# The last two half-width matmuls of an attention decode kernel change places

## The chip, the cores and the metric

The kernel runs on one core of a Trainium2 chip. The metric is the device time of one execution in microseconds (us). A profile comes from one profiled execution; its span is the time from the first to the last instruction, about 2 us less than the device time.

## The reference, cut to what matters

Two attention blocks, A and B, decode one token for four batch rows. A attends to 8192 cached positions, B to the last 2048. Each ends in a projection, and the two results stand side by side.

```python
def _A_ref(x, k_cache, v_cache, wq, wo):            # x: (4, 1, 512), Hq = 32, Hkv = 8, Dh = 128
    q = (x @ wq).reshape(B, Sq, Hq, Dh) ...
    scores = einsum("bhqd,bhkd->bhqk", q, k) * Dh ** -0.5
    o = einsum("bhqk,bhkd->bhqd", softmax(scores), v)
    return o.transpose(0, 2, 1, 3).reshape(B, Sq, Hq * Dh) @ wo
# _B_ref: the same on the last W = 2048 positions
return concatenate([a, b], axis=-1)                  # (4, 1, 1024), bf16
```

## The kernel before

The kernel streams 184.56 MB of keys, values and weights from HBM and works through them in 20 units. The change concerns the very end: the last eight heads (C = 8) of A's projection, whose output is 4 rows of D = 512 columns. The columns are split into two halves of H2 = 256, each accumulated in a PSUM bank of its own. `halves[0]`, called SA in the profile, is copied out by VectorE and sent by SyncE's DMA queue; `halves[1]`, called KT, is copied out by ScalarE and sent by ScalarE's own queue. Every head waits for its own 128 KB piece of the weights (`("WL", i)`).

```python
        halves = [SA[(L + 1) % 2][0:Bn, 0:H2], KTB[2][0:Bn, 0:H2]]
        # ... (cut: seed with the earlier heads' sums, values of the last unit, normalisation)
        for i, n in enumerate(WCH):                  # WCH = [1] * C
            for hq in range(h0, h0 + n):
                for hf in (1, 0):                    # ScalarE's half, then VectorE's
                    def lfn(pe, hq=hq, hf=hf):
                        return pe.matmul(out=halves[hf], lhsT=OT_sb[:, 0, NSEG - 1, hq, :],
                                         rhs=Wl_sb[:, hq, hf * H2:(hf + 1) * H2],
                                         start=False, stop=(hq == C - 1))
                    op("pe", lfn, waits=[("WL", i), ("otr", L), ("oc", L - 1)], inc=("fin", hf) if hq == C - 1 else None)
            h0 += n
        op("dve", lambda dve: dve.tensor_copy(out=osb[:, 0, 0:H2], in_=halves[0]), waits=[("fin", 0)], inc=("ocp", NTURN))
        op("act", lambda act: act.activation(out=osb[:, 0, H2:D], in_=halves[1], func=ACTF.Copy), waits=[("fin", 1)], inc=("Ef",))
        op("act", dma(out[:, 0, H2:D], osb[:, 0, H2:D]), waits=[("Ef",)], inc=("out", 2))
        # ... (cut)
        op("sp", dma(out[:, 0, 0:H2], osb[:, 0, 0:H2]), waits=[("ocp", NTURN)], inc=("out", 0))
        # ... and SyncE's last step: wait for the landing of outputs 1, 2 and 0
```

## Time and profile before

| What | Value |
|---|---|
| device time, first 3 runs | 439.19 us median (438.82 to 439.37) |
| span of the profile | 437.0 us |
| DMA engines at 0.9 or more | 38 of 40 slices |
| start of the last pair of matmuls | 434.47 us |
| last output landed | 436.546 us |

The load stream fills the span; what follows its end, from the last pair of matmuls to the last output's landing, takes 2.07 us. The prediction shows the lines. Three words are used throughout. An **eviction** is the copy of a finished half from its accumulator (PSUM) into SBUF. An **issue** is the instruction by which SyncE or ScalarE hands a transfer to the DMA engines. A transfer reports that it is complete by incrementing a semaphore, a counter on which engines can wait; the last of these increments is its **landing**. Landings are not rows of the timeline: they are read from the trace's record of semaphore increments, to the nanosecond, and so are the starts of packets. From here on the **tail** is the time from the start of the first matmul of the last pair to the last landing of an output. It leaves out when the load stream ends, which differs from run to run.

### The profile page before, as it was taken

What the parts mean: (1) busy time and instruction counts of PE and PEld (TensorE: products, weight loads), DVE (VectorE), ACT (ScalarE), POOL (GpSimd) and SP (SyncE); (2) the same over time, 40 slices, a digit from 0 to 9 for tenths busy, and PEclk for the clock granted to TensorE, in tenths of its full rate; (3) what the DMA queues carried; (4) which work ended last, traced back from release to release, by engine and by line L of the source; (5) the groups of instructions that cost most, each with busy time, mean ns of one, the idle gap of its engine ahead of it and who ended that gap; (6) DMA issues with size and microseconds to landing.
All of it is one profiled execution on the core that took longest, in us unless ns stands there. A gap on an engine that the chain in (4) does not pass through costs nothing.

```text
span 437.0 us, 15525 instructions
## 1 busy us (share of the span) xinstructions
PE 365.0 (84%) x7174; PEld 337.9 (77%) x7184; DVE 210.0 (48%) x406; ACT 195.0 (45%) x249; POOL 27.7 (6%) x88
## 2 busy tenths in 40 slices
PE   0168898998998959895989598969868996989996
PEld 0158897997997949795979588868868886979975
DVE  0004455664564634563456247525643563455651
ACT  1024473573653625371634254434534462536530
POOL 6100000000000000000000000000100000000000
PEclk9999999999999988999999899989996999799999
DMA  8999999999999999999999999999999999999996
GB/s 340 430 421 421 429 412 430 418 439 412 445 432 432 424 438 432 432 432 432 432 432 429 432 432 430 431 433 432 410 454 432 432 432 432 432 432 411 447 407 255
DMA packets 10996, 184.73 MB, mean 423 GB/s; under 512 B 1236, under 2 KB 2280, under 8 KB 2408
## 3 DMA queue, kind: packets, MB, share of 16 engines
q1 hardware_dynamic: 10960, 184.56, 99.1%
q8 instruction: 8, 0.13, 0.1%
q14 instruction: 4, 0.03, 0.0%
q10 hardware_dynamic: 24, 0.01, 0.0%
HBM read 184.56 MB, written 0.01 MB: 422 GB/s over the span
## 4 chain that ended last, share of the span: by engine, by line
PE 54%; DMA 40%; issue 2%; DVE 1%; SPq 1%; ACT 1%
DMA K_sb<-in_A_k_cache_dram 29%; PE KT L283 27%; PE OT L338 11%; DMA K_sb<-in_B_k_cache_dram 7%; PE SB L322 5%; PE SA L322 4%; DMA V_sb<-in_A_v_cache_dram 4%; PE KT L396 4%; PE SA L350 1%; PE KT L338 1%; SPq L566 1%; DVE oacc L404 1%; PE KT L263 1%; ACT KT_sb L299 1%; DVE OS L501 0%
## 5 line engine op out<-in xcount | busy, mean ns | idle before, releaser
L283 PE MATMUL KT<-identf,K_sb 128*128 128x128 f32 x1280 | 207.6, 296 | 44.1 <-DMA K_sb<-in_A_k_cache_dram 30.7
L299 ACT ACTIVATE KT_sb<-KT 128x1024 bf16<-128x1024 bf16 (+1 forms) x192 | 165.1, 881 | 120.6 <-PE KT L283 120.6
L283 PEld LDWEIGHTS KT<-identf,K_sb 128*128 128x128 f32 x1280 | 147.6, 150 | 49.3 <-DMA K_sb<-in_A_k_cache_dram 31.7
L299 DVE COPY KT_sb<-KT 128x512 int32<-128x512 int32 x160 | 110.5, 691 | 132.1 <-PE KT L283 130.7
L338 PE MATMUL OT<-PT,V_sb 128*128 128x64 bf16 x2560 | 78.1, 193 | 1.6 <-issue 1.1
L338 PEld LDWEIGHTS OT<-PT,V_sb 128*128 128x128 bf16 x2560 | 75.9, 98 | 1.8 <-issue 1.2
L469 ACT ACTIVATE PT<-Dt 128x512 bf16<-128x512 f32 x40 | 24.6, 630 | 84.0 <-DVE Dt L458 84.0
L322 PEld LDWEIGHTS SA<-RQc,KT_sb 128*128 128x128 bf16 x1280 | 56.9, 98 | 2.3
L322 PEld LDWEIGHTS SB<-RQc,KT_sb 128*128 128x128 bf16 x1280 | 51.1, 97 | 7.9 <-issue 4.4
L322 PE MATMUL SA<-RQc,KT_sb 128*128 128x16 bf16 x1280 | 56.4, 170 | 0.0
L322 PE MATMUL SB<-RQc,KT_sb 128*128 128x16 bf16 x1280 | 52.9, 170 | 0.0
L420 DVE TENSOR_REDUCE M<-SB 128x8 f32<-128x512 f32 (+1 forms) x20 | 13.8, 692 | 50.0 <-PE SB L322 50.0
L441 POOL PARTITION_ALL_REDUCE MB<-M1m x20 | 7.7, 387 | 334.3 <-DVE M1m L434 334.3
L396 PE MATMUL KT<-Wo_sb,OL 128*4 128x512 bf16 x80 | 18.9, 379 | 0.0
L201 PE MATMUL KT<-ident,x_sb 4*128 4x4 bf16 x8 | 0.6, 170 | 19.9 <-POOL identf L537 19.9
L201 PEld LDWEIGHTS KT<-ident,x_sb 4*128 4x128 bf16 x8 | 0.4, 112 | 20.1 <-issue 20.1
L476 DVE TENSOR_REDUCE LB<-SA 128x8 f32<-128x512 f32 (+1 forms) x20 | 13.7, 684 | 2.8 <-PE SA L350 2.8
L458 DVE TENSOR_TENSOR Dt<-SA,MBm 128x512 f32<-128x512 f32 x20 | 13.8, 692 | 0.7
L367 DVE TENSOR_TENSOR ORx<-KT,MSK 32x1024 bf16<-32x1024 bf16 x10 | 12.1, 1211 | 3.3 <-PE KT L362 3.3
L458 DVE TENSOR_TENSOR Dt<-SB,MBm 128x512 f32<-128x512 f32 x20 | 13.6, 681 | 0.0
L420 DVE TENSOR_REDUCE M<-SA 128x8 f32<-128x512 f32 (+1 forms) x20 | 13.6, 681 | 0.0
L350 PE MATMUL SA<-PT,onesb 128*128 128x128 bf16 x168 | 12.7, 218 | 0.0
(69 smaller groups left out, 118.0 us busy)
## 6 DMA issues: line engine op xcount, KB each, us to landing
K_sb<-in_A_k_cache_dram SPq DMA_DIRECT2D x15, 4096.0 KB, 22.5
V_sb<-in_A_v_cache_dram SPq DMA_DIRECT2D x15, 4096.0 KB, 30.3
K_sb<-in_B_k_cache_dram SPq DMA_DIRECT2D x8, 2048.0 KB, 23.6
V_sb<-in_B_v_cache_dram SPq DMA_DIRECT2D x16, 1024.0 KB, 18.4
V_sb<-in_B_wq_dram SPq DMA_DIRECT2D x1, 4096.0 KB, 12.5
V_sb<-in_A_wq_dram SPq DMA_DIRECT2D x1, 4096.0 KB, 21.8
Wo_sb<-in_B_wo_dram SPq DMA_DIRECT2D x4, 1024.0 KB, 11.9
K_sb<-in_A_k_cache_dram SPq DMA_DIRECT2D x2, 2048.0 KB, 17.5
```

The costliest lines, as they stand in the source:

```text
L283: ins = pe.transpose(out=bkf[:, pi * 128:(pi + 1) * 128], in_=K_sbf[:, slot, t0:t0 + 2, :].rearrange("p t d -> p (t d)"), identity=identf[ ...
L299: ins = e.tensor_copy(out=d, in_=r) if eng == "dve" else e.activation(out=d, in_=r, func=ACTF.Copy)
L322: ins = pe.matmul(out=stb[:, t % NTH * C:(t % NTH + 2) * C], lhsT=ktv[:, pi, :, e], rhs=RQc[:, u % 2, t // TS, e, :], start=(e == 0), stop ...
L338: ins = pe.matmul(out=otb[:, s * NW:s * NW + w], lhsT=V_sb[:, slot, t, :], rhs=PT[:, slot, t * C:t * C + w], start=(j == 0), stop=(j == n ...
L350: ins = pe.matmul(out=SA[u % 2][:, s * NM:(s + 1) * NM], lhsT=onesb[:, :], rhs=PT[:, u % 2, c0:c0 + NM], start=(i == 0), stop=(i == n - 1))
L367: return dve.tensor_tensor(out=ORx[:, :, :, :], in0=bk[0:NR, 0:128].rearrange("p (i o r) -> p r o i", o=1, r=C).broadcast_to([NR, C, C, 12 ...
L396: ins = pe.matmul(out=bk[0:Bn, 0:D], lhsT=OL[:, i, :], rhs=Wo_sb[:, i, :], start=(i == 0), stop=(i == C - 1))
L420: return dve.tensor_reduce(out=M1[:, h * n:(h + 1) * n].rearrange("p (s h) -> p s h", h=C), in_=bank[:, :].rearrange("p (s j h) -> p s h j ...
L441: return pool.partition_all_reduce(MB[:, 0:n], M1m[:, 0:n], channels=128, reduce_op=ReduceOp.max)
L458: return dve.tensor_tensor(out=Dt[:, h * NTH * C:(h + 1) * NTH * C].rearrange("p (s j h) -> p s j h", s=Sh, h=C), in0=bank[:, :].rearrange ...
L469: return act.activation(out=PT[:, u % 2, a:b], in_=Dt[:, a:b], func=ACTF.Exp, scale=scale)
L476: return dve.tensor_reduce(out=LB[:, 0:n].rearrange("p (s h) -> p s h", h=C), in_=SA[u % 2][:, 0:NSEG * NM].rearrange("p (s j h) -> p s h ...
```

## The change

The intent: VectorE's way from accumulator to output is the slower one, so its half should be ready first, ahead of ScalarE's. Only the last head is turned round.

```diff
-                for hf in (1, 0):
+                for hf in (1, 0) if hq < C - 1 else (0, 1):
```

## The prediction

> **What bounds the kernel now.** I read the page first: span, slices, chain.
>
> ```profile
> span 437.0 us, 15525 instructions
> ...
> DMA  8999999999999999999999999999999999999996
> ...
> HBM read 184.56 MB, written 0.01 MB: 422 GB/s over the span
> ...
> PE 54%; DMA 40%; issue 2%; DVE 1%; SPq 1%; ACT 1%
> ```
>
> The DMA engines are at 0.9 or more in 38 of the 40 slices; the two others are the first and the last. So nearly all of the 437 us is the time that 184.56 MB take to arrive. The chain has TensorE in 54% of its steps, but TensorE is paced by those loads. The change touches neither the loads nor anything ahead of the last two matmuls, so the whole argument lies in the last three microseconds. I read those in the timeline from 434.4 us on:
>
> ```profile
> 434.47 0.08 PEld L700 LDWEIGHTS KT<-Wl_sb,OT_sb 128*4 128x4 bf16 x1 [0.23 <-DMA Wl_sb<-in_A_wo_dram]
> 434.47 0.27 PE L700 MATMUL KT<-Wl_sb,OT_sb 128*4 128x256 bf16 x1
> 434.48 0.08 PEld L700 LDWEIGHTS SA<-Wl_sb,OT_sb 128*4 128x4 bf16 x1
> 434.58 0.27 PE L700 MATMUL SA<-Wl_sb,OT_sb 128*4 128x256 bf16 x1
> 434.78 0.37 ACT L705 ACTIVATE osb<-KT 4x256 bf16<-4x256 f32 x1 [9.44 <-PE KT L700]
> 434.89 0.41 DVE L704 CAST osb<-SA 4x256 bf16<-4x256 f32 x1 [2.20 <-PE SA L700]
> 435.18 0.27 ACTq L566 DMA_DIRECT2D out_dram<-osb  x1
> 435.33 0.29 SPq L566 DMA_DIRECT2D out_dram<-osb  x1
> ```
>
> The columns are start, duration, engine, line, operation. KT holds the half of the columns that ScalarE evicts and sends on its own queue; SA holds the half that VectorE evicts and SyncE sends. The last pair of matmuls waits 0.23 us for the last piece of the output weights, so its start is set by the load stream. Then two branches run to the end side by side, the ScalarE one 0.11 us ahead. The chain of waits over the same stretch shows which ends last:
>
> ```profile
> 434.54 0.21 PE KT L700
> 434.74 0.12 PE SA L700
> 434.87 0.02 issue
> 434.89 0.41 DVE osb L704
> ```
>
> It goes through VectorE. The queue's own waits on SyncE close it:
>
> ```profile
> SPq L566 <- DVE osb L704: 7.4, 1, 7.4
> SPq L820 <- DMA out_dram<-osb: 0.9, 1, 0.9
> ```
>
> L820 is the final wait of the program, on both output transfers. SyncE's own issue ends at 435.33 + 0.29 = 435.62, and it then waits 0.9 us, so the outputs have landed near 436.5. The trace's record of semaphore increments gives the two apart: the ScalarE half's last increment at 436.362, the VectorE half's at 436.546. The wait ends at 436.56. The VectorE half is thus last by 0.184 us, and that slack is what a change of order can trade on. From 436.56 to 437.0 comes the closing handshake, the same for both kernels.
>
> **What the Trainium skill says.** Four places bear on it.
>
> "VectorE: DVE Perf Modes", section "The TRN2 errata", gives for PSUM to SBUF 120 + FD cycles at 0.96 GHz on VectorE and 172 + FD at 1.2 GHz on ScalarE. With 256 elements that is an estimate of 392 ns and 357 ns. The trace has 412 and 373: both some 5% longer, and VectorE slower by 39 ns against 35. The page agrees that the VectorE half is the slower one, so it should come first. I use the trace's durations.
>
> "Perfetto Trace Analysis", section "Tensor Engine Instruction (MATMUL, LD_WEIGHTS)", says that a matmul's reported end is computed and not observed. I therefore count from start to start of the evictions. These lie 434.89 − 434.78 = 0.11 us apart, as the matmuls do (434.58 − 434.47).
>
> The same page, section "DMA Instruction — HWDGE (DVE, Sync)", says that the descriptor generator is locked for exclusive use while an instruction generates descriptors, and that the data movement is not in the instruction's profiled window. The trace agrees on the second: an issue of 0.29 us has its last landing 1.2 us after its start. On the first no row of this trace decides: the two issues overlap (435.33 lies before 435.18 + 0.27 = 435.45) and the second takes 0.29 against 0.27.
>
> "DMA: Bandwidth & Descriptors", section "Issuing engines are not separate DMA queues", says that transfers issued from several engines run on the same 16 DMA engines and interleave. In the trace each output is four packets of 512 B, each packet 25 to 28 ns long, in 436.09 to 436.17 for SyncE's queue and 435.94 to 436.03 for ScalarE's. They do not overlap now.
>
> **The change part by part.** It removes nothing and adds nothing. On TensorE one matmul of 256 columns trades places with one other, with the same weights, and the static comparison of the two programs finds the other four engines unchanged. In the last of eight heads the SA matmul now runs first. Their order inside a bank's accumulation does not change, so the result should be bit for bit the same.
>
> The length of each branch, from the start of its eviction to the last landing:
> - VectorE branch: 434.890 to 436.546 = 1.656 us. It is made of 0.412 eviction, 0.029 to the issue (435.33 − 435.30), and 1.215 from the start of the issue to the landing.
> - ScalarE branch: 434.781 to 436.362 = 1.581 us: 0.373 eviction, 0.030 to the issue, 1.178 to the landing.
>
> The VectorE branch is longer by 0.075 us: 0.039 from the eviction and 0.037 from the transfer. Let the first eviction start at t, and the other at t + 0.109. Before, the end is t + 0.109 + 1.656 = t + 1.765 (VectorE), the other at t + 1.581. After, VectorE ends at t + 1.656 and ScalarE at t + 0.109 + 1.581 = t + 1.690. The later of these is t + 1.690, so the end comes 1.765 − 1.690 = **0.075 us earlier**. The whole 0.109 us of matmul spacing is not won, because ScalarE's branch becomes the last one after 0.075.
>
> What else moves: the last matmul of head 6 and the first of head 7 both now write SA, back to back. Before head 7 there is a 0.23 us wait for its weights, far longer than the 0.11 us spacing, so nothing can queue behind that. The accumulators are in separate banks, so VectorE's read of SA runs beside the KT matmul as ScalarE's read of KT runs beside the SA matmul now.
>
> Sum: −0.075 us of 439.19, which is 0.017%. The three runs before lie between 438.82 and 439.37, a spread of 0.55 us, seven times the gain.
>
> **The rivals.** First, **the two issues collide**. Now SyncE's issue begins 0.147 us after ScalarE's (435.331 − 435.184). After the change SyncE's begins at t + 0.441 and ScalarE's at t + 0.512, only 0.071 apart. If the descriptor generator serves one at a time, the second loses up to the added overlap of 0.147 − 0.071 = 0.076 us, which would eat the gain and leave 439.19. The packets would come 0.07 us apart as well, and each queue's four take about 0.09 us on the same DMA engines, a clash of at most 0.02 to 0.03 us. For it: the second issue is already 17 ns longer. Against it: the issues overlap today by 0.12 us with no more than those 17 ns lost. I give this a chance of one in four.
>
> Second, **VectorE stays the last**. If SyncE's transfer takes longer for being first, or its receipt comes late, the end stays on the VectorE branch at up to t + 1.765. To lose the whole gain it would have to lengthen by 0.109 us, for which no row speaks; between 0 and 0.109 us would be gained, so 439.08 to 439.19.
>
> Third, **the load stream decides by itself**. The time at which the last weights land (before 434.47) varies from run to run with 184.56 MB of transfers; 0.1% of the span is already 0.4 us. That does not hang on the order of two matmuls, but it can put the measured median either side of before. This is the likeliest thing to be seen, whatever happens in the tail: 438.8 to 439.4, as the three runs before.
>
> **Range and chances.** Prediction: 439.19 − 0.075, so 439.1 us. The range comes from the noise and not from the mechanism: the spread of 0.55 us over three runs, widened a little for another session, gives 438.5 to 439.7. Two per cent is 8.8 us, and the whole tail after the last matmuls is 2.5 us long; if all of it vanished the verdict would still be "the same". A loss of 2% would need a changed load stream. So faster 0.005, same 0.99, slower 0.005.
>
> **What would show it.** Right, if the timeline has the SA matmul at t' and KT 0.11 us later, the VectorE cast starting first and the ScalarE activation 0.11 us after it; SyncE's issue about 0.07 us ahead of ScalarE's; the ScalarE half's landing now the last, by about 0.03 us; and about 2.02 us from the first of the last pair of matmuls to the end of the final wait, where it is 436.56 − 434.47 = 2.09 now. The span itself may well move the other way. The collision is right if ScalarE's issue instruction is longer than 0.30 us, or its packets start more than 0.76 us after its issue began (435.94 − 435.18 now). The prediction is wrong if that tail is not shorter, or if the time leaves the range, which would point to the load stream.

## The result, and the profile after

The changed kernel takes 439.13 us (median of 6 runs, 438.84 to 439.68), the kernel before in the same rounds 439.11 (6 runs, 438.82 to 439.42). The ratio is 1.0002 with a 95% interval of 0.9989 to 1.0014. A ratio here is the mean time of one kernel's runs over that of the other's of the same rounds, so not quite the ratio of the two medians.

The page of the changed kernel has the same span and the same full DMA row:

```profile
span 437.0 us, 15535 instructions
...
DMA  8999999999999999999999999999999999999996
...
HBM read 184.56 MB, written 0.01 MB: 422 GB/s over the span
```

The timeline of its last microseconds (start, duration, engine, line, operation):

```profile
434.38 0.08 PEld L700 LDWEIGHTS SA<-Wl_sb,OT_sb 128*4 128x4 bf16 x1 [0.24 <-DMA Wl_sb<-in_A_wo_dram]
...
434.49 0.27 PE L700 MATMUL KT<-Wl_sb,OT_sb 128*4 128x256 bf16 x1
434.69 0.41 DVE L704 CAST osb<-SA 4x256 bf16<-4x256 f32 x1 [2.05 <-PE SA L700]
434.80 0.37 ACT L705 ACTIVATE osb<-KT 4x256 bf16<-4x256 f32 x1 [10.20 <-PE KT L700]
435.13 0.29 SPq L566 DMA_DIRECT2D out_dram<-osb  x1
435.20 0.27 ACTq L566 DMA_DIRECT2D out_dram<-osb  x1
```

The order is turned as intended: VectorE starts 0.11 us ahead, and SyncE's issue 0.07 us ahead of ScalarE's. The chain of waits, the last four pieces, now ends on ScalarE:

```profile
434.33 0.32 PE SA L700 x2
434.65 0.12 PE KT L700
434.78 0.02 issue
434.80 0.37 ACT osb L705
```

SyncE's own waits after the change:

```profile
SPq L566 <- DVE osb L704: 7.2, 1, 7.2
SPq L820 <- DMA out_dram<-osb: 1.1, 1, 1.1
```

The last line is what the forecast did not expect. The final wait starts when SyncE's issue is done, at 435.13 + 0.29 = 435.42, and takes 1.1 us, so the outputs have landed near 436.5, as before. The semaphore record has 436.492, against 436.546. That looks like a gain of 0.054 us, but the last pair of matmuls also started earlier, at 434.382 instead of 434.473, because its weights came earlier. The tail is 436.492 − 434.382 = 2.110 us, where it was 436.546 − 434.473 = 2.073. It got **longer by 0.037 us**; the forecast had it shorter by 0.075. One profile each does not tell a mechanism from scatter, so both are repeated first.

### The profile page after: what moved, and what is told of

The parts are those of the page before. It is cut to its first block, busy times and chain, and to the rows that moved or that the text cites. A ratio compares the mean times of both kernels' runs of the same rounds, so it can differ in the third digit from the quotient of the medians.

```text
span 437.0 us, 15535 instructions
## 1 busy us (share of the span) xinstructions
PE 366.5 (84%) x7184; PEld 338.5 (77%) x7184; DVE 209.9 (48%) x406; ACT 195.0 (45%) x249; POOL 27.7 (6%) x88
## 4 chain that ended last, share of the span: by engine, by line
PE 50%; DMA 40%; PEld 4%; issue 2%; DVE 1%; SPq 1%; ACT 1%; PEldq 0%
DMA K_sb<-in_A_k_cache_dram 29%; PE KT L283 25%; PE OT L338 10%; DMA K_sb<-in_B_k_cache_dram 7%; DMA V_sb<-in_A_v_cache_dram 4%; PE SB L322 4%; PE SA L322 4%; PE KT L396 3%; PEld KT L283 2%; PE SA L350 1%; PE KT L338 1%; SPq L566 1%; DVE oacc L404 1%; PEld OT L338 1%; PEld SA L322 1%
```

## The experiments

The two theories at the start. Theory 1: of two outputs sent close together, the later one is held back by the earlier one, and the tighter they come the more; the change brought them closer together. Theory 2: landings scatter by more than the 0.075 us in question.

**The same two kernels again**, no edit.

> The kernel before, once more, for its tail: from the start of the first matmul of the last pair to the last output landing (by the trace's semaphore records). It was 2.073 us in the first profile; the later output (VectorE's half, SyncE's queue) took 1.215 us from issue to landing. Theory 1, the later of two close outputs is delayed by the earlier one, in a repeatable way: 2.05 to 2.10 and 1.20 to 1.23 again. Theory 2, landings scatter from run to run by more than the 0.075 us forecast: the tail moves by over 0.05 us.

> The changed kernel, once more. Its first profile had a tail of 2.110 us, where the prediction had 2.073 - 0.075 = 2.00; the later output (ScalarE's half) took 1.289 us from issue to landing, where it took 1.178 when it was the earlier one. Theory 1 (a repeatable delay of the later output when the issues are only 0.07 us apart): 2.09 to 2.13 and 1.27 to 1.31 again. Theory 2 (scatter): the tail moves by over 0.05 us, towards 2.00. My prediction's step as it stood: 2.00 us and 1.18 us.

Measured: the kernel before has a tail of 2.068 us, the later output 1.211 from issue to landing. The changed kernel has 2.112 and 1.292. Both repeat within 0.005 us, in two profiles each. Theory 2 falls: the 0.04 us are real, and they are a loss. Each kernel from here on was profiled once. What does scatter is the load stream: over these four profiles the last pair starts between 434.38 and 434.64 us.

**A gap between the halves.** To see each branch alone, three matmuls with no use are put between the last two. In the changed kernel the condition is `hf == 0`.

```diff
+                    if hq == C - 1 and hf == 1:
+                        def gfn(pe):
+                            ins = None
+                            for _ in range(3):
+                                ins = pe.matmul(out=KTB[3][:, 0:512], lhsT=ident[:, :], rhs=RQ[0]..., start=True, stop=True)
+                            return ins
+                        op("pe", gfn)
```

> Three matmuls of 512 columns with no use are put between the last two matmuls of the projection (ScalarE's half first), so that the two outputs are some 0.65 us further apart and cannot touch each other. Measured is the branch from the start of VectorE's eviction to its landing. Theory 1: alone it takes 1.60 to 1.62 us, as it did when it was the earlier one in the changed kernel (1.612), not 1.656. Theory 2: anything from 1.56 to 1.68. Prediction's step as it stood: 1.656.

> The same three matmuls, VectorE's half first. Measured is the branch from the start of ScalarE's eviction to its landing. Theory 1: alone it takes 1.57 to 1.60 us, as when it was the earlier one in the kernel before (1.581), so that the pair with a gap shows the changed order ahead by only some 0.03 us (1.612 - 1.581) and not 0.075. Theory 2: anything from 1.53 to 1.70. Prediction's step as it stood: 1.581 and a difference of 0.075.

The timeline of the changed order with the gap shows the two ends apart:

```profile
434.68 0.41 DVE L712 CAST osb<-SA 4x256 bf16<-4x256 f32 x1 [2.09 <-PE SA L700]
...
435.12 0.29 SPq L566 DMA_DIRECT2D out_dram<-osb  x1
...
435.63 0.37 ACT L713 ACTIVATE osb<-KT 4x256 bf16<-4x256 f32 x1 [10.37 <-PE KT L700]
436.04 0.27 ACTq L566 DMA_DIRECT2D out_dram<-osb  x1
```

The issues are 0.92 us apart, which is 0.85 more than in the changed kernel and not 0.65. Alone, VectorE's branch from the start of its eviction to its landing takes 1.616 us (1.617 in the other gap kernel, where it came first) and ScalarE's takes 1.575 in both. From issue to landing the two transfers take the same, 1.177 and 1.172 to 1.173. So both numbers that the forecast used, 1.656 and 1.581, were of branches that met: the first held 0.04 us of waiting for the other output. What separates the branches is the eviction and little else, 0.041 us. With the gap the changed order is ahead by 2.880 − 2.838 = 0.042 us, a little more than the 0.03 expected, and not by 0.075.

It also shows a pattern. In both orders the later output lands a fixed time after the earlier one: 0.184 and 0.183 us in the two profiles of before, 0.188 and 0.187 in those of the changed kernel, although the issues are 0.147 us apart in one and 0.072 in the other. Alone they would land 0.148 and 0.068 us apart. For before that is 0.109 + 1.616 − 1.577, with the 1.577 that ScalarE's branch took as the earlier one in the second profile (1.581 in the first). For the changed kernel it is 0.109 + 1.575 − 1.616. The refined theory 1: the completions of two transfers come no closer than about 0.185 us, and a later one waits that out. This is not a spacing of any two increments: the four that follow the packets of one output come only 0.01 to 0.04 us apart. Taken one by one in their order, those of the later output follow those of the earlier by 0.177 to 0.188 us in these four profiles. Its rival: the second transfer, or ScalarE's, pays a fixed 0.115 us.

**A small delay** separates the two: one matmul of 4 x 192 with no use, between the last two of the changed kernel.

```diff
+                    if hq == C - 1 and hf == 0:
+                        op("pe", lambda pe: pe.matmul(out=KTB[3][0:Bn, 0:192], lhsT=OT_sb[:, 0, NSEG - 1, 0, :], rhs=Wl_sb[:, 0, 0:192],
+                                                      start=True, stop=True))
```

> In the changed kernel one matmul of 4x192 with no use stands between the last two, so that ScalarE's half comes some 0.08 us later. By the first runs an output alone lands 1.177 us after its issue, and of two close ones the later lands 0.183 to 0.188 us after the earlier. Theory 1 (completions are served one after the other, some 0.185 us apart): the later output's landing stays 0.185 us after the earlier one, so the tail to the last landing stays at 2.11 us although the last half is computed 0.08 later, and its time from issue falls from 1.29 to about 1.21. Rival (the delay belongs to ScalarE's queue being second, a fixed 0.115 us): 1.29 from issue again and a tail of 2.19.

```profile
434.81 0.41 DVE L707 CAST osb<-SA 4x256 bf16<-4x256 f32 x1 [2.06 <-PE SA L700]
435.00 0.37 ACT L708 ACTIVATE osb<-KT 4x256 bf16<-4x256 f32 x1 [9.89 <-PE KT L700]
435.25 0.29 SPq L566 DMA_DIRECT2D out_dram<-osb  x1
435.40 0.27 ACTq L566 DMA_DIRECT2D out_dram<-osb  x1
```

ScalarE's eviction now starts 0.19 us after VectorE's, 0.08 more than in the changed kernel. Its output takes 1.205 us from issue instead of 1.29, lands 0.187 after the other, and the tail is 2.107. Delaying the last half by 0.08 us cost nothing: that time had been spent waiting anyway. The fixed charge is out.

**What the later output waits for.** SyncE sends a load of the same shape in place of its output, and the output itself only after ScalarE's has landed.

```diff
-        op("sp", dma(out[:, 0, 0:H2], osb[:, 0, 0:H2]), waits=[("ocp", NTURN)], inc=("out", 0))
+        op("sp", dma(x_sb[0:Bn, 0, 0:H2], X[0][:, 0, 0:H2]), waits=[("ocp", NTURN)], inc=("out", 0))
+        op("sp", dma(out[:, 0, 0:H2], osb[:, 0, 0:H2]), waits=[("out", 2)], inc=("out", 3))
```

> The changed kernel, in which SyncE at the time of its output issues a load of the same shape (four rows of 512 B, from HBM to SBUF) in its place, and sends VectorE's half only after ScalarE's has landed (the result stays right, the end comes over 1 us later). Measured is ScalarE's output from issue to landing. If what holds it back is any earlier transfer on the same DMA engines that is not complete: 1.25 us or more, as behind an output (1.29). If it is the earlier write to HBM: near 1.18 as when alone.

```profile
435.35 0.27 SPq L566 DMA_DIRECT2D x_sb<-in_A_x_dram  x1
435.42 0.27 ACTq L566 DMA_DIRECT2D out_dram<-osb  x1
436.85 0.28 SPq L566 DMA_DIRECT2D out_dram<-osb  x1
```

The load lands 1.305 us after its issue, and ScalarE's output 1.420 after its own, which is 0.187 us after the load. Each transfer makes four increments after its packets, as many as it has rows; taken one by one, those of the output follow those of the load by 0.180 to 0.187. So the earlier transfer need not be a write to HBM: a load that is not complete holds the output back as another output does. The packets of the two run among each other here. The output's last one starts only 0.029 us after the load's last (436.340 and 436.311), and its landing still comes 0.187 after, so most of the distance arises after the packets.

**One transfer for both halves**, from ScalarE's queue, in either order.

```diff
-        op("act", dma(out[:, 0, H2:D], osb[:, 0, H2:D]), waits=[("Ef",)], inc=("out", 2))
+        op("act", dma(out[:, 0, 0:D], osb[:, 0, 0:D]), waits=[("Ef",), ("ocp", NTURN)], inc=("out", 2))
```

(SyncE's output transfer and the wait for it are taken out.)

> The changed order, but one output transfer of 4 KB, issued by ScalarE's queue when both halves are evicted, in place of two of 2 KB. Theory 1: no second completion to wait for, so issue to landing 1.18 to 1.21 and a tail of 2.00 to 2.03 us from the first matmul of the last pair to the last landing, some 0.05 us less than before (2.07) and 0.1 less than the changed kernel (2.11). Rival (it is the bytes or the rows that take the time, not the second completion): 1.29 and a tail of 2.11.

> The order of before with the same single transfer from ScalarE's queue. The issue now waits for VectorE's eviction, which ends last: 0.109 + 0.412 against 0.109 + 0.373 after the first eviction's start. Theory 1: tail 2.04 to 2.07 us, 0.04 longer than after_one: with one transfer the change of order is worth the 0.039 us by which the evictions differ. Rival as for after_one: 2.15.

This one missed. In the changed order the tail is 2.073 us and not 2.00 to 2.03: the transfer of four rows of 1 KB takes 1.254 us from issue to landing, 0.08 more than one of four rows of 512 B. There is no second completion, but the wider rows cost nearly as much: from the start of the first packet to the end of the last it is 0.167 us (436.053 to 436.220), where an output of 2 KB took 0.094 (435.940 to 436.034 in the first profile of before). It is level with the kernel before and 0.037 us better than the changed kernel. In the order of before the tail is 2.169, where 2.04 to 2.07 were expected and 2.15 by the rival. Of the 0.096 us more than the other order, 0.039 are the evictions' difference, as expected; the rest is that ScalarE's queue has the wait for VectorE as a step of its own: VectorE is done at 435.472, and the issue starts at 435.564.

**Uneven halves.** If completions need 0.185 us between them, it pays to let the first half end earlier, at the price of a longer second one, up to the point where the second one arrives just in time. VectorE's half becomes 208 of the 512 columns in the changed order, and 272 in the order of before.

```diff
-        halves = [SA[(L + 1) % 2][0:Bn, 0:H2], KTB[2][0:Bn, 0:H2]]
+        CUT = [0, 208, D]                     # [0, 272, D] in the order of before
+        halves = [SA[(L + 1) % 2][0:Bn, 0:CUT[1]], KTB[2][0:Bn, 0:D - CUT[1]]]
```

(and CUT in place of H2 in the matmuls, evictions and transfers)

> The changed order with VectorE's half cut to 208 columns and ScalarE's widened to 304. Estimate from the runs: a column costs 0.42 ns in the matmul (0.109 us for 256), and in the evictions about 1.04 ns on VectorE and 0.83 on ScalarE. VectorE's landing then comes 48 x 1.46 = 0.070 us earlier, at 1.85 us after the start of the first matmul of the last pair, and the later completion can follow it by 0.185, at 2.037; ScalarE's output alone would land at 2.110 - 0.115 + 48 x 0.83/1000 = 2.035. Theory 1 (completions at least 0.185 us apart): a tail of 2.03 to 2.05, the later output 1.18 to 1.20 from its issue, so 0.03 below before (2.07) and 0.07 below the changed kernel (2.11). Rival (a fixed delay of 0.115 for ScalarE's transfer as the second): 2.15. In the time, 0.03 us can't be seen: ratio 1.000 within its interval.

> The order of before, with ScalarE's half cut to 240 columns and VectorE's widened to 272. Theory 1: ScalarE's landing 16 x 1.25 = 0.020 us earlier, at 1.865 after the start of the first matmul of the last pair, the later one at 1.865 + 0.185 = 2.05, and VectorE's alone at 2.031 + 0.017 = 2.048: a tail of 2.05, 0.02 below before. Rival (VectorE's branch sets the end by its own length): 2.07 + 0.017 = 2.087.

Measured: tails of 2.056 and 2.052 us. The order of before, recut, came out as estimated (2.05), with landings 0.190 apart, although VectorE's last half is now the wider one. The other is 0.006 over its range: its landings are 0.211 apart, and the later output took 1.196 us from its issue. This does not speak against the spacing, which is a least distance: ScalarE's output was hardly held back. Its rows are of 608 B. Between the 1.172 of 512 B and the 1.254 of 1 KB that gives an estimate of 1.19 from issue to landing alone, and the forecast had left out that wider rows take longer. In the other kernel the later output took 1.177, as when alone. So in both the later half now arrives about when it may, which was the aim; neither tests the 0.185 further. The rivals' 2.15 and 2.087 are both out. In time, the 208-column kernel is 439.10 us (median of 5) beside 439.22 of before (median of 9), ratio 0.9996, interval 0.9983 to 1.0010: the same. In one profile it has a shorter tail than both kernels, and I do not claim more.

All intervals together (us, in order of landing; "apart" is from the earlier landing to the later):

| Run | earlier output, issue to landing | later output, issue to landing | apart | tail |
|---|---|---|---|---|
| before | ScalarE 1.178 | VectorE 1.215 | 0.184 | 2.073 |
| before, again | ScalarE 1.173 | VectorE 1.211 | 0.183 | 2.068 |
| changed | VectorE 1.173 | ScalarE 1.289 | 0.188 | 2.110 |
| changed, again | VectorE 1.177 | ScalarE 1.292 | 0.187 | 2.112 |
| before, gap | ScalarE 1.173 | VectorE 1.177 | 0.997 | 2.880 |
| changed, gap | VectorE 1.177 | ScalarE 1.172 | 0.913 | 2.838 |
| changed, small delay | VectorE 1.173 | ScalarE 1.205 | 0.187 | 2.107 |
| changed, load first | load 1.305 | ScalarE 1.420 | 0.187 | not comparable |
| changed, 208 columns | VectorE 1.169 | ScalarE 1.196 | 0.211 | 2.056 |
| before, 272 columns | ScalarE 1.171 | VectorE 1.177 | 0.190 | 2.052 |

## Why the prediction was right or wrong

**The time**: 439.13 us against 439.1 forecast, inside the range. The reason given, that the load stream sets the time and its scatter hides the tail, holds. The last pair starts between 434.38 and 434.64 us in four profiles of the two kernels, while their tails differ by 0.04. That 439.13 lies so near to 439.1 is luck and says nothing for the 0.075: any small change of the tail, of either sign, would have fallen into the range.

**The order of events** was right: SA first, VectorE's cast 0.11 us ahead, SyncE's issue 0.07 us ahead, ScalarE's half the last to land. So the second rival, that VectorE's half stays the last, is out.

**The gain in the tail** was wrong in sign. The step that failed is "The later of these is t + 1.690, so the end comes 1.765 − 1.690 = 0.075 us earlier". It takes the two branches' lengths as measured in one order and adds them up in the other, as if they did not touch. VectorE's 1.656 held 0.04 of waiting (alone 1.616), nearly all of it in the 0.037 that the forecast put down to the transfer, and ScalarE's 1.581 became 1.692 when it came second. What the runs show in its place: at this spacing the end is the earlier landing plus 0.185. Before, with ScalarE's first, that is 1.577 + 0.184 = 1.761 after the first eviction's start. After, with VectorE's first, it is 1.616 + 0.187 = 1.803. The profiles have 1.765 and 1.800. So the quicker branch should go first here, and the change put the slower one there. That ScalarE's half would be last "by about 0.03 us" failed with it: it is last by 0.188. By the prediction's own sign, a tail that is not shorter, this part is wrong: to the end of the final wait it is 2.132 us, where before had 2.116 and 2.02 were forecast.

**The first rival, the collision,** was the right idea at a wrong size and in a wrong place. It allowed a loss of up to 0.076 us and left the time where it was. The later output lost some 0.115 (1.289 against 1.172 to 1.178). Of the two signs named for a collision, the first did not show: ScalarE's issue instruction took 0.274 us, as when alone (0.273). SyncE's took 0.289 as the first and 0.289 alone, so the 17 ns counted for this rival were no loss either. The second sign did show: ScalarE's packets start 0.787 us after its issue instead of 0.756, which is 0.03 of the loss. Whether the descriptor generator or the packets ahead kept them, no run shows. The other 0.085 came after them, up to the landing. The packet clash that I put at 0.02 to 0.03 at most could cover only the first part.

**What the mechanism is** inside the DMA engines, the runs do not show; they show that a transfer's completion comes some 0.18 to 0.19 us or more after that of an earlier, incomplete one, a load included. The Trainium skill, "DMA: Bandwidth & Descriptors", section "Queues, rings and completion order", says that the semaphore increment is a strongly ordered write that lands only after every earlier write from that DMA engine, across its queues. If the rows of SyncE's and ScalarE's transfers share engines, that would keep the later completion behind the earlier one whichever queue it came from. It fits the order that all runs show. But the page gives no time for it, so it does not tell why the distance is 0.18 us, and no run here put the two transfers on different engines or on one queue. This cause is argued and not shown.

**The part of the loss that shows in the span** is smaller. From the start of the last pair to the end of the last instruction it is 2.572 and 2.568 us before, 2.587 and 2.590 after: 0.018 us more instead of 0.04. After the last landing the program ends in 0.499 and 0.500 us before and in 0.477 and 0.478 after. The traces show where the 0.02 lie. SyncE's final wait (L820) ends 0.043 and 0.045 us after the last landing before, where that is SyncE's own output, and 0.022 and 0.023 after it in the changed kernel; from there to the end it is 0.455 to 0.456 us in all four. Why the wait ends sooner was not tested. I had also read 436.56 as the end of the final wait of before; it is the start of a record 0.027 us long; and the chain's 54% for TensorE are a share of the span, not of the steps.

## What to carry to other kernels

The two small transfers that end this program are not independent branches: measure each alone before adding them up in another order. Here the one that is ready soonest should go first, and the halves may be cut so that the second arrives just when the first is done. But before tuning a tail of 2 us, look at what sets its start. In a kernel that waits on its load stream, a change of 0.04 us lies far below the scatter of the stream's end, and only intervals inside the profile can tell it from nothing.

## What the Trainium skill lacked or had wrong

- "DMA: Bandwidth & Descriptors" tells that transfers from several issuing engines interleave on the same DMA engines, and orders their increments, but gives no spacing of completions. Here the later of two close transfers of 2 KB landed 0.183 to 0.188 us after the earlier one in all six runs that had such a pair, one of them behind a load.
- The same page, section "Latency and other measured facts", puts the HWDGE first byte at about 600 ns and the smallest HBM round trip at about 800 ns. Here an output of 2 KB, alone, has its first packet 0.754 to 0.760 us after the start of its issue and lands after 1.172 to 1.177 us. So the first packet comes some 0.15 us later than the page's first byte, if the two are counted alike; the round trip is a least time, which the landing does not contradict.
- "VectorE: DVE Perf Modes", section "The TRN2 errata", gives cycles that make an estimate of 392 ns (VectorE) and 357 ns (ScalarE) for these evictions of 256 columns from PSUM, with its perf-mode divisor at 1. Measured are 411 to 412 and 372 to 374, some 5% more.
